# An FNet layer plus MLP on one core: shorter warm products and a re-cut opening, and two DFT weight matrices loaded in 256-byte rows

## Chip, core and metric

The kernel runs on one core of a Trainium2 chip. The metric is the device time of one execution in microseconds (us). The engines are TensorE (PE, with its weight loads shown apart as PEld), VectorE (DVE), ScalarE (ACT), GpSimd (POOL) and SyncE (SP), which here only issues DMAs.

## What is computed

The input x is 2048 rows of 640 columns. It is normalised row by row, and the normalised rows go two ways whose results are added to x:

```
xn = layernorm(x)                                   # no weights, over 640 columns
a, b = xn @ hid_re.T, xn @ hid_im.T                 # hid: 640 x 640
y  = seq_re @ a - seq_im @ b                        # seq: 2048 x 2048
out = x + y + gelu(xn @ w1 + b1) @ w2 + b2          # w1: 640 x 1536, w2: 1536 x 640
```

All data are 32-bit floats.

## The kernel before, in words

**Products.** Nearly every matrix product is made of three: each operand is split into a high part (`fp32r`, a copy on ACT) and a low part (what is left, a subtraction on DVE), and high x high, high x low and low x high are added up in PSUM (L278 to L280; in the first layer of the MLP L304). The helper `split` (L154 to L161) writes both parts. One product has 128 x 128 weights and 512 moving columns.

**The order** is written out by hand: the program text is each engine's order, and each engine, SP included, goes through its list without overtaking. A tile is waited for by semaphores that the language sets.

**The stages.** The MLP runs first, over blocks of 512 rows. The loop over g (L1051) goes through twelve hidden units of 128 columns for block 0 and twelve for block 1, with `hidden(g)` (15 products into bank g % 3), `gelu(g)` (ACT and DVE) and `output(g)` (15 products into five banks). Blocks 2 and 3 follow with a scheme that saves products (`head`, `mid`, `finish`), and then the sequence and hidden DFTs with another such scheme (from L1453 on).

**The opening (L653 to L771).** Four row tiles x0 to x3 of 128 x 640 are loaded, two by SP and two by ACT. PE meanwhile multiplies a zero tile (`warm_up`, L675, `NWARM` times, and once more later). For tiles 0 and 2 DVE finds the mean (`ln_stats`), for 1 and 3 ACT sums the rows (`sum_on_act`). `center` (L704) subtracts the mean into `xp`. PE transposes `xp` in pieces of 128 x 128 (`transpose_x`, L691) into five banks `tacc[j]`, one for each 128 columns; a bank is full when all four tiles have put their quarter there. `split` then makes `XT[j]` from bank j: its high part on ACT (L160), its low part on DVE (L161). w1's first unit, `W1[0]`, is split in two column parts (L726 to L729), its second, `W1[1]`, by `prep_w1(1)`. Then PE does `hidden(0)`, its 15 steps in the order of `FIRST` (a step (j, k): column piece j; k = 0 is high x high, 1 uses the low part of XT, 2 the low part of W1), and `hidden(1)`, with the steps that need W1's low part last. `hidden(2)` lets four transposes of `wide` (the row scales) run after its first step (L762 to L766).

**The DFT weights wr and wi (hid_re, hid_im).** They are taken in five column chunks j. `load_w(m, j)` (L378) loads chunk j of matrix m with four DMAs of 128-byte rows, `turn_w` (L390) transposes the 32 x 32 blocks on DVE into a tile `wt`, and `put_w` (L402) splits sums of it and stores them to DRAM through POOL's queue, for use much later. Chunks 0 and 1 (`WEARLY` = 2) are handled in the second MLP block, in six steps `prep_w(0)` to `prep_w(5)` after units 0 to 5 (`w_early`, L1048): chunk 0 is loaded at the end of the first block (`open_w`, L962), chunk 1 by `prep_w(0)`. `ZT` (L224) is a pair of 512-column buffers, which hold transposed rows of block 1 until `prep_xt` (L242) has split them (i = 9, L1077 to L1081) and rows of block 2 from `second_block(3)` on (L1001).

Of the kernel before, what the change touches and what calls it, by code (L numbers as in the profile page):

```python
# [15 lines left out]
P = 128  # L16
Q = 4
B = 32
EPS = 1e-5
NWARM = 10  # L20
# [6 lines left out]
def kernel(  # L27
# [261 lines left out]

    def hidden(g, aside=None):  # L290
# [4 lines left out]
        if g == 0:  # L295
            steps = FIRST
        if g == 1:

            steps.sort(key=lambda s: s[1] == 2)
        for n, (j, k) in enumerate(steps):  # L300
            if aside and n == ASIDE:
                aside()
            a, b = kinds[k]
            nc.tensor.matmul(  # L304
                acc, W1[i][:, a, j * P : (j + 1) * P], XT[j][:, b], start=n == 0, stop=n == len(steps) - 1
            )
# [70 lines left out]

    def load_w(m, j):  # L378

        if A["w"]:  # L380
            t = A["w"].tile([P, EB, B], F32, tag=f"wraw{m}", bufs=1, name=f"wraw{m}_{j}")
        else:
            t = A["wz"][:, m].rearrange("p (e b) -> p e b", b=B)
        A["wraw", m] = t
        v = (wr, wi)[m].rearrange("(n r) d -> r n d", r=B)
        for q in range(Q):
            s0 = q * DQ + j * B
            nc.sync.dma_start(t[q * B : (q + 1) * B], v[:, :, s0 : s0 + B])

    def turn_w(m, j):  # L390
        if A["w"]:
            t = A["w"].tile([P, D], F32, tag=f"wt{m}", bufs=1, name=f"wt{m}_{j}")
        else:
            t = A["wz"][:, 2 + m]
        A["wt", m] = t
        nc.vector.transpose(
            t.rearrange("p (c q i) -> p q c i", q=Q, i=B),
            A.pop(("wraw", m)).rearrange("p (q c) i -> p q c i", q=Q),
        )
# [20 lines left out]
    def prep_w(s):  # L420
# [4 lines left out]
        if k == 0:  # L425
            turn_w(0, j)
            turn_w(1, j)
            if j + 1 < ND and j != WEARLY - 1:
                load_w(0, j + 1)
                load_w(1, j + 1)  # L430
# [234 lines left out]
    nc.vector.memset(zeros, 0.0)  # L665
    warm = whole["as"][:, :TB]
    nc.vector.tensor_copy(warm, zeros)  # L667
# [3 lines left out]
    load_w1(1, cuts=(0, 2, ND))  # L671
# [3 lines left out]
    def warm_up():  # L675
        nc.tensor.matmul(wacc, warm[:, :P], warm, start=True, stop=True)  # L676
# [3 lines left out]
    load_w1(2)  # L680
# [41 lines left out]
    center(2, ALU.subtract, MV[:, 2, 0:1])  # L722
    sum_on_act(3)
    center(3, ALU.add, MV[:, 3, 5:6], 0, 2)
    center(3, ALU.add, MV[:, 3, 5:6], 2, ND)
    for lo, hi in ((0, 2 * P), (2 * P, D)):  # L726
        h, l = (W1[0][:, k, lo:hi] for k in range(2))
        nc.scalar.activation(h, first_w1[:, lo:hi], AF.Copy)
        nc.vector.tensor_tensor(l, first_w1[:, lo:hi], h.bitcast(F32), op=ALU.subtract)  # L729
# [12 lines left out]
    acc0 = hidden(0)  # L742
    prep_w1(1)
    acc1 = hidden(1)
# [188 lines left out]
    def first_block(i):  # L933
# [20 lines left out]
        if i == 10:  # L954
            load_xo(0)
            ln_scale(8, 4)
# [5 lines left out]
    def open_w():  # L962
# [4 lines left out]
        load_w(0, 0)  # L967
        load_w(1, 0)
# [15 lines left out]
    def second_block(i):  # L984
# [12 lines left out]
        if i == 3:  # L997
            A["zs"] = place("xc01", (P, 30 * P), F32, name="zs")
# [802 lines left out]
```

## Time and profile before

| | us |
|---|---|
| time, median of 3 runs (lowest to highest) | 851.04 (850.51 to 851.35) |
| time of the profiled execution | 850.46 |
| its span, first to last instruction | 848.7 |
| around the span | 1.8 |
| PE busy | 841.7 |
| DVE busy | 666.8 |
| ACT busy | 356.0 |

A time in the trace counts from the start of the span. A row of the timeline gives the start, the length and the engine, then line, operation, names and shape, a count where equal instructions follow one another, and in brackets how long the engine had been idle and what ended that. A row of a queue (SPq) gives the time in which DMAs were issued, not their transfer. A row of groups ends in the busy time, the mean length in ns, and the idle time before them.

### The profile page before, as it was taken

To read this page: it belongs to the slowest core of one execution; us is meant where nothing else is said; L and a number is where in the kernel's file an instruction comes from. 1 tells how busy PE (TensorE), PEld (TensorE's weight loads), DVE (VectorE), ACT (ScalarE), POOL (GpSimd) and SP (SyncE) were. 2 spreads that over 40 slices of the span, in tenths; PEclk is the share of its full clock that TensorE was granted. 3 is DMA by queue.
4 is the path that set the end of the run, shared out by engine and by line. 5 is a ranking of instruction groups with operands and counts; after the bars stand their busy time and mean duration, and the time that the engine had idled before them with its cause. 6 is when DMAs were issued, how large, how long until landed. Compare 5 with 4: busy or idle time off the path is not lost.

```text
span 848.7 us, 10340 instructions
## 1 busy us (share of the span) xinstructions
PE 841.7 (99%) x3707; PEld 695.2 (82%) x3707; DVE 666.8 (79%) x841; ACT 356.0 (42%) x499; POOL 48.9 (6%) x70
## 2 busy tenths in 40 slices
PE   9999999999999999999999999999999999999997
PEld 7888888878888888888888888888888888888886
DVE  6665766776758888779988887889967898885687
ACT  7454534456665555343444344232323433223241
POOL 0000311031221400000000000000000000000001
PEclk9999999999999999999999999999999999999999
DMA  6667699837679989858644679663865779705464
GB/s 182 192 184 188 159 228 252 193 87 189 202 245 355 358 186 174 173 132 188 152 137 111 162 229 289 151 150 98 205 168 169 253 191 229 306 19 180 124 172 108
DMA packets 207491, 158.45 MB, mean 187 GB/s; under 512 B 81040, under 2 KB 180880, under 8 KB 206928
## 3 DMA queue, kind: packets, MB, share of 16 engines
q1 hardware_dynamic: 198752, 135.25, 62.7%
q0 software_dynamic: 4144, 21.24, 6.3%
q10 hardware_dynamic: 4544, 1.31, 0.6%
q8 instruction: 29, 0.48, 0.3%
q14 instruction: 22, 0.18, 0.1%
HBM read 114.76 MB, written 42.99 MB: 186 GB/s over the span
## 4 chain that ended last, share of the span: by engine, by line
PE 99%; DVE 0%; issue 0%
PE banks L278 29%; PE banks L279 29%; PE banks L280 29%; PE banks L304 10%; PE banks L676 1%; PE banks L693 0%; PE banks L336 0%; PE banks L339 0%; PE banks L337 0%; DVE yo L1766 0%; DVE zeros L665 0%; DVE as L667 0%; PE banks L764 0%
## 5 line engine op out<-in xcount | busy, mean ns | idle before, releaser
L278 PE MATMUL banks<-as,xab 128*128 128x512 f32 x411 | 159.9, 389 | 0.0
L280 PE MATMUL banks<-as,xab 128*128 128x512 f32 x411 | 159.9, 389 | 0.0
L279 PE MATMUL banks<-as,xab 128*128 128x512 f32 x411 | 159.9, 389 | 0.0
L160 ACT ACTIVATE as<-r 128x1024 fp32r<-128x1024 f32 x80 | 85.0, 1062 | 178.1 <-PE banks L280 149.7
L161 DVE TENSOR_TENSOR as<-r,as 128x1024 fp32r<-128x1024 f32 x80 | 97.2, 1216 | 41.5 <-ACT as L160 41.5
L278 PEld LDWEIGHTS banks<-as,xab 128*128 128x128 f32 x411 | 77.1, 188 | 16.1
L279 PEld LDWEIGHTS banks<-as,xab 128*128 128x128 f32 x411 | 77.1, 188 | 16.0
L280 PEld LDWEIGHTS banks<-as,xab 128*128 128x128 f32 x411 | 77.1, 188 | 16.0
L278 PE MATMUL banks<-as,xc 128*128 128x512 f32 x224 | 87.1, 389 | 0.0
L279 PE MATMUL banks<-as,xc 128*128 128x512 f32 x224 | 87.1, 389 | 0.0
L280 PE MATMUL banks<-as,xc 128*128 128x512 f32 x224 | 87.1, 389 | 0.0
L160 ACT ACTIVATE as<-rt 128x1024 fp32r<-128x1024 f32 x32 | 34.0, 1062 | 70.5 <-PE banks L280 62.5
L304 PE MATMUL banks<-xtt,xab 128*128 128x512 f32 x240 | 57.1, 391 | 0.0
L304 PEld LDWEIGHTS banks<-xtt,xab 128*128 128x128 f32 x240 | 44.7, 188 | 9.8 <-ACT xtt L160 0.4
L278 PEld LDWEIGHTS banks<-as,xc 128*128 128x128 f32 x224 | 42.0, 188 | 8.8
L279 PEld LDWEIGHTS banks<-as,xc 128*128 128x128 f32 x224 | 42.0, 188 | 8.7
L280 PEld LDWEIGHTS banks<-as,xc 128*128 128x128 f32 x224 | 42.0, 188 | 8.7
L161 DVE TENSOR_TENSOR as<-rt,as 128x1024 fp32r<-128x1024 f32 x32 | 38.8, 1211 | 5.3 <-ACT as L160 5.3
L160 ACT ACTIVATE as<-u 128x1024 fp32r<-128x1024 f32 (+1 forms) x24 | 22.1, 920 | 48.2 <-PE banks L280 48.2
L512 DVE STREAM_TRANSPOSE r<-raw 128x1024 f32<-128x1024 f32 x32 | 39.5, 1240 | 3.1 <-PE banks L280 2.6
L161 DVE TENSOR_TENSOR as<-u,as 128x1024 fp32r<-128x1024 f32 (+1 forms) x24 | 24.9, 1042 | 18.8 <-ACT as L160 18.8
L512 DVE STREAM_TRANSPOSE rt<-raw 128x1024 f32<-128x1024 f32 x32 | 38.8, 1230 | 0.9 <-PE banks L280 0.8
(352 smaller groups left out, 1618.5 us busy)
## 6 DMA issues: line engine op xcount, KB each, us to landing
raw<-in_A_dft_seq_re_dram SPq DMA_DIRECT2D x64, 256.0 KB, 5.6
raw<-in_A_dft_seq_im_dram SPq DMA_DIRECT2D x64, 256.0 KB, 5.0
ws<-wit SPq DMA_DIRECT2D x15, 384.0 KB, 5.4
xs<-x SPq DMA_DIRECT2D x64, 80.0 KB, 1.8
xo<-in_A_x_dram SPq DMA_DIRECT2D x16, 320.0 KB, 6.7
xab<-wit SPq DMA_DIRECT2D x13, 384.0 KB, 4.2
wit<-wstp POOLq DMA_DIRECT2D x12, 384.0 KB, 3.7
x<-in_A_x_dram SPq DMA_DIRECT2D x14, 320.0 KB, 4.4
```

Of the source, the lines that this page charges most:

```text
L160: nc.scalar.activation(h, s, AF.Copy)
L161: nc.vector.tensor_tensor(l, s, h.bitcast(F32), op=ALU.subtract)
L278: nc.tensor.matmul(acc, wh, mh, start=first, stop=False, skip_group_check=goes_on)
L279: nc.tensor.matmul(acc, wh, ml, start=False, stop=False, skip_group_check=goes_on)
L280: nc.tensor.matmul(acc, wl, mh, start=False, stop=last, skip_group_check=goes_on)
L304: nc.tensor.matmul(acc, W1[i][:, a, j * P : (j + 1) * P], XT[j][:, b], start=n == 0, stop=n == len(steps) - 1)
L512: nc.vector.transpose(held(pieces[g][2], u).rearrange("p c (n i) -> p c n i", i=B), r.rearrange("p n (c i) -> p c n i", i=B))
L676: nc.tensor.matmul(wacc, warm[:, :P], warm, start=True, stop=True)
```

## The change

It has two parts that have nothing to do with each other.

**The opening.**

- The zero tile of the warm products is 128 x 128 instead of 128 x 512, stays an ordinary f32 tile (the `fp32r` copy on DVE is gone), and the products are 128 x 128 x 128. There are twelve instead of ten.
- Tiles 2 and 3 are centered in two column parts each (columns of pieces 0 and 1, then 2 to 4), alternating, with the split of W1[0]'s first part between them. The split of W1[0]'s second part stands between the splits of XT[1] and XT[2].
- PE transposes tiles 2 and 3 by turns for pieces 0 and 1.
- `hidden(0)` and `hidden(1)` become `first_two`: the same 30 products into the same two banks, but two of W1[0]'s last steps (those that need the low parts of XT[3] and XT[4]) stand behind the first steps of W1[1], and in FIRST some steps change place.
- w1's second unit is loaded with four DMAs instead of eight, the third with eight instead of four.

**The DFT weights.** Chunks 0 and 1 of each matrix come together, as rows of 64 columns (256 bytes). Of wi the first 16 of 20 row blocks go into ZT, behind `load_xo(0)` in `first_block(10)`; the rest, and wr, into new tiles in `open_w`. `turn_two` transposes a chunk in five pieces instead of two instructions; for chunk 1 it moves from `prep_w(3)` to the start of `second_block(3)`.

```
-NWARM = 10
+NWARM = 12
...
-    nc.vector.memset(zeros, 0.0)
-    warm = whole["as"][:, :TB]
-    nc.vector.tensor_copy(warm, zeros)
+    nc.vector.memset(zeros[:, :P], 0.0)
...
-    load_w1(1, cuts=(0, 2, ND))
+    load_w1(1)
...
-        nc.tensor.matmul(wacc, warm[:, :P], warm, start=True, stop=True)
+        nc.tensor.matmul(wacc[:, :P], zeros[:, :P], zeros[:, :P], start=True, stop=True)
...
-    load_w1(2)
+    load_w1(2, cuts=(0, 2, ND))
...
-    FIRST = [(0, 0), (0, 2), (1, 0), (1, 2), (0, 1), (2, 0), (2, 2), (1, 1), (3, 0), (3, 2)]
-    FIRST += [(2, 1), (4, 0), (4, 2), (3, 1), (4, 1)]
+    FIRST = [(0, 0), (0, 2), (1, 0), (1, 2), (0, 1), (2, 0), (1, 1), (3, 0), (2, 2), (3, 2)]
+    FIRST += [(4, 0), (4, 2), (2, 1), (3, 1), (4, 1)]
...
+    def first_two():
+        kinds = ((0, 0), (0, 1), (1, 0))
+        second = sorted(((j, k) for j in range(ND) for k in range(3)), key=lambda s: s[1])
+        order = [(0, s) for s in FIRST[:13]] + [(1, s) for s in second[:2]]
+        order += [(0, FIRST[13]), (1, second[2]), (0, FIRST[14])] + [(1, s) for s in second[3:]]
...
-    center(2, ALU.subtract, MV[:, 2, 0:1])
     sum_on_act(3)
-    center(3, ALU.add, MV[:, 3, 5:6], 0, 2)
-    center(3, ALU.add, MV[:, 3, 5:6], 2, ND)
-    for lo, hi in ((0, 2 * P), (2 * P, D)):
+    def split_first(lo, hi):
         h, l = (W1[0][:, k, lo:hi] for k in range(2))
         nc.scalar.activation(h, first_w1[:, lo:hi], AF.Copy)
         nc.vector.tensor_tensor(l, first_w1[:, lo:hi], h.bitcast(F32), op=ALU.subtract)
+    def centers(j0, j1):
+        center(2, ALU.subtract, MV[:, 2, 0:1], j0, j1)
+        center(3, ALU.add, MV[:, 3, 5:6], j0, j1)
+    centers(0, 2)
+    split_first(0, 2 * P)
+    centers(2, ND)
     transpose_x(0, 0, ND)
     transpose_x(1, 0, ND)
     warm_up()
-    for j0, j1 in ((0, 2), (2, ND)):
-        transpose_x(2, j0, j1)
-        transpose_x(3, j0, j1)
+    for j in range(2):
+        transpose_x(2, j, j + 1)
+        transpose_x(3, j, j + 1)
+    for c in (2, 3):
+        transpose_x(c, 2, ND)
     for j in range(ND):
         split(XT[j][:, 0], XT[j][:, 1], tacc[j])
+        if j == 1:
+            split_first(2 * P, D)
...
-    acc0 = hidden(0)
     prep_w1(1)
-    acc1 = hidden(1)
+    acc0, acc1 = first_two()
...
+    def load_two(m, k0=0):
+        v = (wr, wi)[m].rearrange("(n r) d -> r n d", r=B)
+        for t, n0, n1 in TWO[m][k0:]:
+            for q in range(Q):
+                nc.sync.dma_start(t[q * B : (q + 1) * B], v[:, n0:n1, q * DQ : q * DQ + 2 * B])
...
+            TWO[1] = [(ZT.rearrange("p a (e b) -> p (a e) b", b=2 * B), 0, WCUT)]
+            load_two(1)
```

The first place is DVE's list at the opening (`x_114` to `x_120` are x0, x2 and x3; `xab_122` is W1[0] and then W1[1], `xtt` is XT). Before:

```order
L665 MEMSET zeros 128x512
L667 CAST as<-zeros 128x512
...
L705 TENSOR_SCALAR xp<-x_118,mv 128x4x5x32
L705 TENSOR_SCALAR xp<-x_120,mv 128x4x2x32
L705 TENSOR_SCALAR xp<-x_120,mv 128x4x3x32
L729 TENSOR_TENSOR xab_122<-w1r_139,xab_122 128x256
L729 TENSOR_TENSOR xab_122<-w1r_139,xab_122 128x384
L161 TENSOR_TENSOR xtt<-banks,xtt 128x512 x5
```

Changed:

```order
L700 MEMSET zeros 128x128
...
L738 TENSOR_SCALAR xp<-x_118,mv 128x4x2x32
L738 TENSOR_SCALAR xp<-x_120,mv 128x4x2x32
L760 TENSOR_TENSOR xab_122<-w1r_138,xab_122 128x256
L738 TENSOR_SCALAR xp<-x_118,mv 128x4x3x32
L738 TENSOR_SCALAR xp<-x_120,mv 128x4x3x32
L161 TENSOR_TENSOR xtt<-banks,xtt 128x512 x2
L760 TENSOR_TENSOR xab_122<-w1r_138,xab_122 128x384
L161 TENSOR_TENSOR xtt<-banks,xtt 128x512 x3
```

The columns of pieces 0 and 1 of x2 and x3 are centered back to back, and the second half of W1[0] stands inside the five splits of XT.

The second place is ACT's list at the same point. Before:

```order
L728 ACTIVATE xab_122<-w1r_139 128x256
L728 ACTIVATE xab_122<-w1r_139 128x384
L160 ACTIVATE xtt<-banks 128x512 x5
L160 ACTIVATE xab_122<-w1r_148 128x640
L702 ACTIVATE ab,mv<-xp 128x640 x2
```

Changed:

```order
L759 ACTIVATE xab_122<-w1r_138 128x256
L160 ACTIVATE xtt<-banks 128x512 x2
L759 ACTIVATE xab_122<-w1r_138 128x384
L160 ACTIVATE xtt<-banks 128x512 x3
L160 ACTIVATE xab_122<-w1r_147 128x640
L735 ACTIVATE ab,mv<-xp 128x640 x2
```

Here too the second half of W1[0] moves between XT[1] and XT[2].

The third place is SP's list around the change of block. Before:

```order
L363 DMA xo_842<-in_A_x_dram 32x16x160 x4
L203 DMA xs<-x_657 32x640 x4
...
L388 DMA wraw_0_919<-in_A_dft_hid_re_dram 32x20x32 x4
L388 DMA wraw_0_924<-in_A_dft_hid_im_dram 32x20x32 x4
...
L234 DMA z_1018<-xs 32x16x160 x4
L388 DMA wraw_1_1033<-in_A_dft_hid_re_dram 32x20x32 x4
L388 DMA wraw_1_1038<-in_A_dft_hid_im_dram 32x20x32 x4
L203 DMA xs<-x_873 32x640 x4
```

Changed:

```order
L376 DMA xo_844<-in_A_x_dram 32x16x160 x4
L399 DMA zt<-in_A_dft_hid_im_dram 32x16x64 x4
L203 DMA xs<-x_659 32x640 x4
...
L399 DMA wrest<-in_A_dft_hid_im_dram 32x4x64 x4
L399 DMA wraw<-in_A_dft_hid_re_dram 32x10x64 x8
...
L234 DMA z_1028<-xs 32x16x160 x4
L203 DMA xs<-x_879 32x640 x4
```

Four DMAs into ZT stand ahead of the stores of the normalised rows (`xs`), twelve instead of eight at the end of the block, and the eight behind `z` are gone.

More of the change, by code (lines that the diff above doesn't have):

```diff
@@ L288, in unit @@
         return g if g < NF else LATE[g % NF]
+    def first_two():
[3 more added lines that the diff above has]
+        order += [(0, FIRST[13]), (1, second[2]), (0, FIRST[14])] + [(1, s) for s in second[3:]]
+        for g, (j, k) in order:
+            a, b = kinds[k]
+            ends = FIRST if g == 0 else second
+            nc.tensor.matmul(
+                bank(g),
+                W1[g][:, a, j * P : (j + 1) * P],
+                XT[j][:, b],
+                start=(j, k) == ends[0],
+                stop=(j, k) == ends[-1],
+            )
+        return bank(0), bank(1)
     def hidden(g, aside=None):
@@ L390, in turn_w @@
     def turn_w(m, j):
[L391 to L395, printed above, removed]
+        t = A["wt", m] = A["wz"][:, 2 + m]
         nc.vector.transpose(
@@ L424, in prep_w @@
             return
-        if k == 0:
+        if k == 0 and j == 0:
+            turn_two(1, j)
+            turn_two(0, j)
+        if k == 0 and j >= WEARLY:
             turn_w(0, j)
             turn_w(1, j)
-            if j + 1 < ND and j != WEARLY - 1:
+            if j + 1 < ND:
                 load_w(0, j + 1)
@@ L966, in open_w @@
         A["wst"] = A["w"].tile([P, 12 * P], F32R, name="wst")
-        load_w(0, 0)
-        load_w(1, 0)
+        t = A["w"].tile([P, EB, 2 * B], F32, name="wraw")
+        TWO[0] = [(t[:, : EB // 2], 0, EB // 2), (t[:, EB // 2 :], EB // 2, EB)]
+        TWO[1].append((A["w"].tile([P, EB - WCUT, 2 * B], F32, name="wrest"), WCUT, EB))
+        load_two(1, 1)
+        load_two(0)
     def open_tw():
```

27 lines of the change are left out of this document (19 added, 8 removed).

## Prediction

> **What bounds the kernel now.** I read the page first: which engine is busy, and what the chain that ended last is made of.
>
> ```profile
> PE 841.7 (99%) x3707; PEld 695.2 (82%) x3707; DVE 666.8 (79%) x841; ACT 356.0 (42%) x499; POOL 48.9 (6%) x70
> PE 99%; DVE 0%; issue 0%
> ```
>
> PE is busy for all but 7 us of 848.7, and the chain hardly leaves it. So an edit moves the time only where PE waits, or where it works slowly. The second view is the list of what PE's weight loads waited for, over the whole run (total, times, longest):
>
> ```profile
> PEld banks L676 <- DVE as L667: 1.9, 1, 1.9
> PEld banks L693 <- issue: 0.6, 1, 0.6
> PEld banks L304 <- ACT xtt L160: 0.4, 2, 0.2
> PEld banks L278 <- ACT banks L857: 0.3, 1, 0.3
> PEld banks L278 <- DVE banks L452: 0.3, 1, 0.3
> PEld banks L279 <- DVE xtt L161: 0.3, 1, 0.3
> PEld banks L304 <- ACT xab L160: 0.2, 1, 0.2
> ```
>
> That is all: 3.1 us in the opening (L676, L693, L304) and 0.9 us at the start of the later blocks (L278, L279). None of these names a load of wr or wi (`wraw`) or a transpose of them (`wt`). So the half of the change on the DFT weights can hardly gain; it can only cost, if it makes a new wait. What there is to gain stands in the opening. The third view is PE's timeline there:
>
> ```profile
> 1.91 4.63 PE L676 MATMUL banks<-as 128*128 128x512 f32 x10 [1.91 <-DVE as L667]
> 6.42 1.66 PE L693 MATMUL banks<-ident,xp 128*128 128x128 f32 x7
> 8.48 1.14 PE L693 MATMUL banks<-ident,xp 128*128 128x128 f32 x9
> 9.66 7.46 PE L304 MATMUL banks<-xtt,xab 128*128 128x512 f32 x31
> 16.96 0.60 PE L764 MATMUL banks<-ident,ab 128*128 128x128 f32 x4
> ```
>
> Ten warm products take 4.63, so 0.43 each (the last one's tail lies beyond). Then come transposes: seven in 1.66, over 0.2 apart; from 8.48 on nine in 1.14, 0.11 apart. **PE doubles its pace near 7.8**, 5.9 us after its first product, in the middle of the first ten transposes. The real products begin at 9.66 and run 0.23 apart; 30 of them would take 6.8, and the 31st, which opens `hidden(2)`, starts 0.23 before the transposes at 16.96, at 16.73. So only some 0.27 is lost among the 30, and the rest of the opening's price is the 9.66 us before them. That date, and the losses behind it, are what the first half of the change can move.
>
> **The opening, step by step.** DVE and ACT there, and the lengths of the centering parts from the rows by form:
>
> ```profile
> 0.91 0.48 DVE L665 MEMSET zeros<- 128x512 f32 x1 [0.91 <-PEq L1787]
> 1.43 0.43 DVE L667 CAST as<-zeros 128x512 fp32r<-128x512 f32 x1
> 5.72 0.56 DVE L705 TENSOR_SCALAR xp<-x,mv 128x640 f32<-128x640 f32 x1
> 7.38 1.15 DVE L705 TENSOR_SCALAR xp<-x,mv 128x640 f32<-128x640 f32 x3
> 9.03 0.56 DVE L729 TENSOR_TENSOR xab<-w1r,xab 128x384 fp32r<-128x384 f32 x1 [0.16 <-ACT xab L728]
> 9.63 3.08 DVE L161 TENSOR_TENSOR xtt<-banks,xtt 128x512 fp32r<-128x512 f32 x5
> ```
>
> ```profile
> L705 DVE TENSOR_SCALAR xp<-x,mv 128x384 f32<-128x384 f32 x1 | 0.4, 415 | 0.0
> L705 DVE TENSOR_SCALAR xp<-x,mv 128x256 f32<-128x256 f32 x1 | 0.3, 349 | 0.0
> ```
>
> ```profile
> 8.47 0.53 ACT L728 ACTIVATE xab<-w1r 128x384 fp32r<-128x384 f32 x1 [0.77 <-DMA w1r<-in_B_w_dram]
> 9.01 2.56 ACT L160 ACTIVATE xtt<-banks 128x512 fp32r<-128x512 f32 x5
> 9.01 0.60 ACT L160 ACTIVATE xtt<-banks 128x512 fp32r<-128x512 f32 x1
> 12.42 0.74 ACT L160 ACTIVATE xab<-w1r 128x640 fp32r<-128x640 f32 x1 [0.86 <-DMA w1r<-in_B_w_dram]
> ```
>
> *Start.* The memset is a quarter as wide; between nothing saved (0.48) and a quarter (0.12) I take 0.15, and the 0.43 of the cast goes. PE starts near 1.15 instead of 1.91, **0.75 earlier**.
>
> *Twelve short warm products.* The trace has no f32 product of 128 columns. The nearest rows bound it: a transpose of that shape (0.21 at the slow pace) and the product of 512 columns (0.43). I take 0.43: a transpose only moves data, and already takes twice as long per column as the 512-column product (0.43/512), so a true f32 product lies above it. Twelve then end near 1.15 + 5.15 = 6.3, where the first transposes can start anyway (x0 is centered at 5.72 + 0.56 = 6.28). At 0.21 they end at 3.7 and PE idles for 2.7: that is the second rival. The Trainium skill, page "FP8 and Floating Point Precision", section "TensorE Precision Notes", gives true FP32 four passes; 4 x 128 columns would be as long as the 512 of before, and the sum would stay as it is.
>
> *First ten transposes.* They start at 6.42 as before. What they take depends on when the pace doubles. I assume that the date follows PE's first work, so 0.75 earlier, near 7.05: then three transposes go at 0.21 and seven at 0.11 and end 0.35 earlier, and with the same product between (L676 there too) the second batch can start at **8.13 instead of 8.48**. Its input is ready: tile 2's and 3's first parts are centered by 7.38 + 0.35 + 0.35 = 8.08 at the latest.
>
> *First high part.* In before it starts at 9.01, 0.53 after 8.48. Bank 0 is now full after the second transpose of the batch instead of the third, 0.11 sooner: 8.55. The first product follows 0.65 later as before (9.66 - 9.01): **9.20 instead of 9.66**. W1[0]'s second half, which held ACT until 9.0, no longer stands ahead.
>
> *New stall.* That half (0.53) now stands between the high parts of XT[1] and XT[2]. High parts are 0.49 apart ((2.56 - 0.60) / 4), so XT[2]'s is ready 0.49 + 0.49 + 0.53 + 0.60 = 2.1 after the first one's start. The sixth product needs it and could start at 0.65 + 5 x 0.23 + 0.11 = 1.9, where 0.11 is what a first product after a wait loses (two starts at 9.66 and 9.99 in the trace, 0.1 over the usual 0.23). So PE waits 0.2 and loses 0.1 again. DVE does as much work as before, in another order; its last low part ends near 12.7 as it did (9.63 + 3.08), and two steps that need the last low parts now stand at places 16 and 18, behind it. W1[1] comes sooner, since the wait of 0.86 at 12.42 was for its DMAs:
>
> ```profile
> 1.65 11.02 SPq L256 DMA_DIRECT2D w1r<-in_B_w_dram  x20
> w1r<-in_B_w_dram SPq DMA_DIRECT2D x4, 80.0 KB, 2.0
> ```
>
> Each issue takes 0.5, so four fewer ahead bring it 2 us forward; it is there when ACT comes to it, near 11.5.
>
> *Sum.* From the first product: 6.8 + 0.2 + 0.2 = 7.2 (before 7.07). `hidden(2)` starts at 9.20 + 7.2 = **16.4 instead of 16.73: 0.3 us saved.** If the doubling stays at 7.8, the start is 9.55 and the sum 16.75: nothing. If it comes before 6.4, centering is the limit (second batch at 7.8 for piece 0 of tile 2, 8.1 for tile 3) and 0.5 is saved.
>
> *Does it last?* Behind the opening the next that could be late are the row scales (`wide`) and the first unit's gelu:
>
> ```profile
> 16.09 0.62 ACT L755 ACTIVATE ab<-mv 128x512 f32<-128x512 f32 x1
> 19.58 0.63 ACT L326 ACTIVATE hs<-ab 128x512 fp32r<-128x512 f32 x1
> 20.59 0.39 PE L336 MATMUL banks<-hs,rt 128*128 128x512 f32 x1
> ```
>
> `wide` ends at 16.71, 0.25 ahead of its use, and `hs` at 20.21, 0.38 ahead of PE. Both hang on ACT's list, which gains by W1[1] coming up to 0.9 earlier, so they move along. From there PE is never idle until the 0.9 us of the later blocks, and those waits hang on work that PE itself releases. So 0.3 of the opening is 0.3 at the end.
>
> **The DFT weights.**
>
> ```profile
> 86.65 1.92 SPq L363 DMA_DIRECT2D xo<-in_A_x_dram  x4
> 95.00 7.36 SPq L203 DMA_DIRECT2D xs<-x  x16
> 104.77 4.32 SPq L388 DMA_DIRECT2D wraw<-in_A_dft_hid_re_dram  x4
> ```
>
> ```profile
> 87.39 0.69 DVE L161 TENSOR_TENSOR xtt<-zt,xtt 128x512 fp32r<-128x512 f32 x1 [0.19 <-ACT xtt L160]
> 111.70 0.84 DVE L396 STREAM_TRANSPOSE wt<-wraw 128x640 f32<-128x640 f32 x1 [3.83 <-DMA wraw<-in_A_dft_hid_re_dram]
> 114.22 0.85 DVE L396 STREAM_TRANSPOSE wt<-wraw 128x640 f32<-128x640 f32 x1 [1.68 <-DMA wraw<-in_A_dft_hid_im_dram]
> ```
>
> The DMAs into ZT must wait until its last reader is done (87.39 + 0.69 = 88.1). On SP the `xs` stores are queued behind them, which start only at 95.0, when DVE has their rows. So 88.1 + 4 issues of 0.5 to 1.1 (1.92 / 4; 4.32 / 4) ends by 92.5: hidden in SP's idle 6 us. At the end of the block, twelve issues with half as many rows for the same bytes replace eight, and DVE's waits (3.8 and 1.7) can only shrink or grow by an us or two. ACT and DVE wait there, PE doesn't: nothing. Six more transposes of small size cost DVE some 0.5 for two chunks, beside PE's products: nothing. In the second block eight issues (8.4 us of SP) go, which lets `xs` and `z` of the last block come earlier; no wait of PE hangs on them: nothing. Cost of the whole half: 0, and 1 to 2 us if the cover in SP's queue were gone.
>
> **The sum against the time.** The profiled execution took 850.46, so the change gives 850.15 on its footing. The median shown is 0.6 above that execution. The Trainium skill, page "TensorE: Matmul & The Clock Gate", section "Part 1: The HAM clock gate", says that the pace doubles at the edge of a free-running window of 3.4 us, so at another date in each run; by it the first rival would hold in some runs and the 0.5 in others. One trace cannot show that: it has one doubling, 5.9 us after PE's start. I cannot tell whether the median's 0.6 stays, take half of it, and forecast **850.4**.
>
> **Rivals.** (1) *No gain*: the doubling stays at 7.8, or ACT's inserted half costs more than 0.2. `hidden(2)` then starts at 16.7 to 16.9 and the time is that of before, 850.5 to 851.1. For it speaks that only one trace shows the doubling; against it that PE starts 0.75 earlier. (2) *Slower, by the warm products*: if one takes only 0.21, they end at 3.7, PE idles for 2.7, and the doubling, 5.9 after the next work at 6.42, comes at 12.3. From 9.8 on the products would run at 0.43 for 2.5 us, a loss of 1.25; the transposes lose 0.5 more. The time is 852.2. It decides from a doubling later than the first product, 9.6. Against it: the argument on the length above. (3) *Slower, by SP's queue*: the DMAs into ZT hold up the `xs` stores after all and PE meets a wait of 1 to 3 us at the head of the later blocks: 852.5. Against it: 2.5 us of room, and no wait of PE near. (4) *Much faster* would need all of PE's later waits to go: 850.15 - 0.9 = 849.2, and even that is within the bound below.
>
> **How the numbers follow.** About 0.2% (1.7 us) is what a measurement of this kernel can tell from no change. Forecast with its spread (saving 0 to 0.8) 0.65, no gain 0.22, rival 2 0.08, rival 3 0.03, faster than all I can name 0.02. Both of the first two and 0.02 of rival 2 are within the bound: same 0.89; slower 0.09; faster 0.02. The range for 8 in 10 takes the forecast from its best case (0.5 saved, and 0.3 for the medians: 849.7) to the upper end of no gain with some spread: 851.4.
>
> **What would show it.** PE's first product at 1.1 to 1.2; twelve warm products 0.43 apart; the first product of W1[0] at 9.2; a gap of some 0.2 before the sixth; `hidden(2)` at 16.4; PE's waits from there on the same three. Warm products at 0.2, or slow transposes behind 8.5, would prove the forecast wrong, and so would a wait of PE on `z`, `xs` or `wt`.

## Result: 1.3 us slower, and two halves that cost nothing alone

The changed kernel takes 851.96 us (median of 14 runs, 850.71 to 854.75), the kernel before 850.67 (14 runs, 850.29 to 852.14): a ratio of 1.0018, 95% interval 1.0011 to 1.0025. Forecast was 850.4. The runs of the changed kernel spread over 4 us, those of before over less than 2; this spread turns out to be part of the answer.

The profiled run took 853.18 (span 851.4) and is one of the longer ones. PE's timeline in the opening, changed kernel:

```profile
1.04 5.49 PE L709 MATMUL banks<-zeros 128*128 128x128 f32 x24 [1.04 <-DVE zeros L700]
6.44 1.48 PE L726 MATMUL banks<-ident,xp 128*128 128x128 f32 x10
7.98 1.60 PE L726 MATMUL banks<-ident,xp 128*128 128x128 f32 x10
9.34 7.09 PE L299 MATMUL banks<-xtt,xab 128*128 128x512 f32 x30
16.27 0.40 PE L317 MATMUL banks<-xtt,xab 128*128 128x512 f32 x1
```

`hidden(2)` starts at 16.27 instead of 16.73; forecast was 16.4. What PE's weight loads waited for over the whole run (the five longest: total, times, longest), and the page's busy times and chain:

```profile
PEld banks L278 <- ACT hs L339: 1.1, 1, 1.1
PEld banks L709 <- DVE zeros L700: 1.0, 1, 1.0
PEld banks L279 <- DVE hs L341: 0.9, 1, 0.9
PEld banks L317 <- ACT xab L160: 0.9, 1, 0.9
PEld banks L317 <- DVE xab L161: 0.6, 1, 0.6
```

```profile
PE 843.3 (99%) x3722; PEld 696.5 (82%) x3722; DVE 666.3 (78%) x847; ACT 355.4 (42%) x499; POOL 48.9 (6%) x70
PE 84%; DMA 6%; DVE 3%; SPq 2%; issue 2%; ACT 2%; POOL 0%; ACTq 0%; DVEq 0%; POOLq 0%
```

Behind the opening the waits for `hs` and `xab` are new, and the chain that ended last, 99% PE before, now leaves PE for 16% of the span. Read the count behind PE too: 3722 records instead of 3707. The two places in PE's timeline:

```profile
30.97 2.31 PE L317 MATMUL banks<-xtt,xab 128*128 128x512 f32 x7 [0.46 <-ACT xab L160]
151.35 0.50 PE L278 MATMUL banks<-hs,r 128*128 128x512 f32 x1 [0.65 <-ACT hs L339]
152.43 0.50 PE L279 MATMUL banks<-hs,r 128*128 128x512 f32 x1 [0.58 <-DVE hs L341]
```

From start to start, PE lost 1.1 us in `hidden(4)` near 31 and 1.8 at 151. With the 0.46 gained, and what else differs along the run, the last product ends 2.7 later than in before's profile (846.27 instead of 843.56), as much as the two profiled times differ.

*The first place.* W1[4], which `hidden(4)` needs, is split on ACT behind gelu work that follows the split of W1[3], and that one waits for a DMA. ACT's timeline, first of before, then of the changed kernel:

```profile
21.39 0.74 ACT L160 ACTIVATE xab<-w1r 128x640 fp32r<-128x640 f32 x1 [0.70 <-DMA w1r<-in_B_w_dram]
29.48 0.72 ACT L160 ACTIVATE xab<-w1r 128x640 fp32r<-128x640 f32 x1
```

```profile
22.11 0.74 ACT L160 ACTIVATE xab<-w1r 128x640 fp32r<-128x640 f32 x1 [2.15 <-DMA w1r<-in_B_w_dram]
30.19 0.72 ACT L160 ACTIVATE xab<-w1r 128x640 fp32r<-128x640 f32 x1
```

PE came 0.46 earlier, the DMA 0.7 later, and W1[4] follows the DMA: 29.48 became 30.19.

*The second place.* `hs` at 151 is a unit's gelu result; ACT makes its high part behind three copies into `wst`, the buffer from which chunk 1 of wr and wi is stored. ACT's timeline, before, then changed:

```profile
141.88 0.42 ACT L160 ACTIVATE wst<-wt 128x256 fp32r<-128x256 f32 x1 [2.00 <-DMA wit<-wst]
144.56 0.63 ACT L326 ACTIVATE hs<-ab 128x512 fp32r<-128x512 f32 x1
```

```profile
147.27 0.42 ACT L160 ACTIVATE wst<-wt 128x256 fp32r<-128x256 f32 x1 [6.31 <-DMA wit<-wst]
150.67 0.63 ACT L339 ACTIVATE hs<-ab 128x512 fp32r<-128x512 f32 x1
```

A store must end before its buffer is written again; ACT stood 6.31 us for it instead of 2.00. What shared the DMA engines with it stands in the list of issues of SP, from 124 us on in before, then from 129 us on in the changed kernel:

```profile
124.12 6.00 SPq L388 DMA_DIRECT2D wraw<-in_A_dft_hid_re_dram  x4
130.23 2.39 SPq L388 DMA_DIRECT2D wraw<-in_A_dft_hid_im_dram  x4
132.72 10.72 SPq L203 DMA_DIRECT2D xs<-x  x16
144.90 2.24 SPq L234 DMA_DIRECT2D z<-xs  x4
```

```profile
129.71 8.79 SPq L203 DMA_DIRECT2D xs<-x  x16
140.91 1.92 SPq L234 DMA_DIRECT2D z<-xs  x4
142.88 2.27 SPq L845 DMA_DIRECT2D rq<-in_B_w_dram  x4
```

In before the two stores of chunk 1, issued at 138.3 and 138.9, take 3.5 and 4.3 us, and z comes behind them. In the changed kernel they are issued at 141.7 and 142.2, while z is issued (140.9 to 142.8) and ahead of rq (142.9), and take 5.5 and 7.1.

### The profile page after: what moved, and what is told of

Its sections match the earlier page's. It is cut to its first block, busy times and chain, and to the rows that moved or that the text cites. A ratio compares the mean times of both kernels' runs of the same rounds, so it can differ in the third digit from the quotient of the medians.

```text
span 851.4 us, 10375 instructions
## 1 busy us (share of the span) xinstructions
PE 843.3 (99%) x3722; PEld 696.5 (82%) x3722; DVE 666.3 (78%) x847; ACT 355.4 (42%) x499; POOL 48.9 (6%) x70
## 4 chain that ended last, share of the span: by engine, by line
PE 84%; DMA 6%; DVE 3%; SPq 2%; issue 2%; ACT 2%; POOL 0%; ACTq 0%; DVEq 0%; POOLq 0%
PE banks L279 27%; PE banks L278 27%; PE banks L280 27%; PE banks L317 2%; DMA x<-in_A_x_dram 2%; DMA wit<-wst 2%; SPq L256 1%; DMA w2r<-in_B_w_dram 1%; DMA xs<-x 1%; SPq L203 0%; ACT ab L335 0%; DVE st L185 0%; DVE x L201 0%; DVE zt L238 0%; DMA w1r<-in_B_w_dram 0%
## 5 line engine op out<-in xcount | busy, mean ns | idle before, releaser
L317 PE MATMUL banks<-xtt,xab 128*128 128x512 f32 x210 | 50.4, 391 | 0.6 <-ACT xab L160 0.5
L317 PEld LDWEIGHTS banks<-xtt,xab 128*128 128x128 f32 x210 | 39.2, 188 | 9.5 <-ACT xab L160 0.9
```

What stands on the lines that cost most here:

```text
L317: nc.tensor.matmul(acc, W1[i][:, a, j * P : (j + 1) * P], XT[j][:, b], start=n == 0, stop=n == len(steps) - 1)
```

## The experiments

Thirteen kernels ran; none changes what is computed, and where one adds work it is said. Times are medians beside runs of the kernel before on the same chip.

### Each half alone, and the queue held

`opening_only` keeps the opening and undoes the DFT half, `dft_only` the reverse. `held_queue` is the changed kernel, but `prep_w(0)` loads chunk 1 once more, over itself, with sixteen DMAs for the bytes of the eight that went (extra work), and `turn_two` for chunk 1 waits for them.

```
 opening_only: DFT part of the diff undone
 dft_only:     opening part of the diff undone
 held_queue:   + in prep_w(0): chunk 1 loaded once more, sixteen DMAs
```

> The kernel before with the whole edit of the opening and nothing of the edit on wr and wi. Theory A (the loss comes from the wr/wi half, in the second block): the saving of the opening (0.45 us at hidden(2) in the profile of the changed kernel) stays at least in part, 850.2 to 850.6 against 850.7 of before, and no wait of PE near 150 us. Theory B (the loss comes from the opening, which brings PE to the first units before their weights are there): PE waits about 1 us for W1 near 30 us, and the time is 851 to 852.

> The kernel before with the whole edit on wr and wi and nothing of the opening. Theory A: 851.2 to 852.2, with a wait of PE for a hidden unit (hs) near 148 to 150 us. Theory B: 850.7, as before, with no such wait.

> The changed kernel; at the place where chunk 1 was loaded before, chunk 1 of both matrices is loaded once more over itself, in 128-byte rows (16 DMAs, the bytes of the eight that the change removed). It adds work. Theory A with the freed queue as cause (z and w1 for the last blocks now load on top of the stores of the split weights, so ACT waits 6.3 instead of 2.0 us for a store, and PE for ACT): the stores land in 3 to 4 us again, ACT's wait near 141 us falls to 2, the wait of PE near 150 us goes, and the time is 850.3 to 851.2. If the freed queue is not the cause (the loads into ZT and the late chunk 0 are): the time stays at 852 or goes above it.

| run | this | before | ratio (95%) |
|---|---|---|---|
| opening_only | 850.64 | 850.48 | 1.0003 (0.9995 to 1.0012) |
| dft_only | 850.57 | 850.48 | 1.0002 (0.9993 to 1.0011) |
| held_queue | 855.79 | 850.48 | 1.0060 (1.0047 to 1.0073) |

Neither half alone costs anything that can be measured, so neither theory holds by itself: the two halves act together, though they were described as having nothing to do with each other. How, is seen in the slack of that `hs`: the time from the end of its low part (DVE) to the moment at which PE would start that unit's output. The low part is needed by the second product, 0.23 later, so a slack of -0.1 or -0.2 costs PE next to nothing. It is 3.5 us in before, 1.7 with the opening alone, -0.1 with the DFT half alone, -1.8 with both. The opening eats 1.8, the DFT half 3.6, together 5.3 of 3.5: in these four traces they add up, and only the sum crosses zero.

`held_queue` missed, and is no clean test: its stores did fall to 3.1 and 3.5 us, but the repeated loads became something to wait for, near 144, and PE paid twice (last section).

### What in the opening delays the second block

In the runs with the opening, DVE waits for x8, the first tile of the next block (in `held_queue` and `dft_newwarm` for x9). DVE's timeline with the opening alone:

```profile
80.66 0.89 DVE L185 BATCH_NORM_STATS2 st<-x 128x6 f32<-128x320 f32 x2 [1.27 <-DMA x<-in_A_x_dram]
```

In before that row starts at 79.27 without a wait. At the same time the list of DMA queues for a window shows a packet of 16 KB on the queue for instructions (last figure: its share of the 16 engines' time). For 77.0 to 79.6 with the opening alone, and for 79.8 to 82.0 in before:

```profile
q8 instruction: 1, 0.02, 2.5%
```

```profile
q8 instruction: 1, 0.02, 2.8%
```

2.5% of 16 engines over 2.6 us is one engine busy for 1.0 us. In before that window of 77.0 to 79.6 has no such packet: the fetch comes at 80.5, in the opening's run at 78.5. There are 29 such packets in a run, and PE has 2 x 3707 records of matmuls and weight loads, 256 for each packet. The Trainium skill, page "Perfetto Trace Analysis", section "Per-instruction lifecycle: what the profiler-reported window actually captures", says that an instruction has 64 bytes; 256 of them are 16 KB, so the trace agrees with fetches of PE's list.

The trace doesn't name the engine of a packet, so that the fetch and x8 share one is argued, not seen. A count fits it: packets under 512 B come sixteen in each 0.8 us from 79.7 to 81.3 with the opening alone, but fifteen from 78.1 to 78.9 and fifteen from 78.9 to 79.7, as if one of sixteen engines were held while the fetch runs.

The short f32 products lengthen that list: twelve products, and the one between the transposes, are 26 records of matmuls where eleven were, each with its weight load: 30 instructions more, and the 257th is reached 15 pairs, or 3.4 us at 0.227 each, earlier. That is **theory C**: the fetches move by 2 to 3 us and meet x8 instead of x11. (In the traces with the longer list the one near 80 comes 1.2 to 3.0 earlier than in before.) Theory D puts the delay to the re-ordered loads and splits.

`dft_newwarm` is `dft_only` plus the new warm products; `after_oldwarm` is the changed kernel with the old ones.

```
 dft_newwarm (on dft_only)              after_oldwarm (on the changed kernel)
-NWARM = 10                            -NWARM = 12
+NWARM = 12                            +NWARM = 10
-nc.vector.memset(zeros, 0.0)          -nc.vector.memset(zeros[:, :P], 0.0)
-nc.vector.tensor_copy(warm, zeros)    +nc.vector.memset(zeros, 0.0)
+nc.vector.memset(zeros[:, :P], 0.0)   +nc.vector.tensor_copy(warm, zeros)
 and the product's operands alike
```

> The run with the DFT half alone, and from the opening only the new warm products (short memset, no cast, twelve f32 products of 128 columns). In the runs so far hs of the unit near 150 us ended 3.5 us ahead of its use in before, 1.7 with the opening alone, 0 with the DFT half alone and 1.8 too late with both: two delays that add up and cross zero only together. Theory C says that the opening's share of that delay comes from its warm products: an f32 product takes two weight loads and two matmuls in the trace, so PE's list is longer, and each fetch of instructions (about 1 us of one DMA engine) comes 1.5 to 2.5 us earlier and falls into the load of x8 instead of x11. Then here: a fetch near 78.5 rather than 80.1, x8 landing over 1 us later than in the run with the DFT half alone (78.82), a wait of PE for hs near 150 of 1 us or more, and 851.2 to 852.0. Theory D says that the opening's share comes from the loads and splits that it re-orders (w1's units, SP's list): then the fetch may move, but x8 lands near 79, no wait over 0.3 near 150, and 850.3 to 850.8.

> The changed kernel with the warm products of before (memset of 512 columns, the copy to fp32r, ten products of 512 columns), all the rest of the change kept. Theory C: the fetches of instructions go back to where they were (one near 80 to 80.5 instead of 79.2), x8 lands near 79 to 79.5 instead of 81.42, the wait for hs near 150 is 0.3 us or nothing instead of 1.7, and the time is 850.5 to 851.0. Theory D (the re-ordered loads do it): x8 lands after 80.5, the wait near 150 stays over 1 us, and the time is 851.7 to 852.2.

`dft_newwarm` 851.99 (850.65 to 854.16), ratio 1.0015 (1.0006 to 1.0024); `after_oldwarm` 850.17 (849.97 to 850.50), ratio 0.9995 (0.9986 to 1.0004); before 850.70. **Beside the DFT half, the warm products carry the loss**: put into that half, which costs nothing by itself, they bring it; taken out of the changed kernel, it goes, and the spread with it. (Without the DFT half they cost nothing: `opening_only` has them.) In `dft_newwarm` it is x9 that comes late, not x8 as I had expected. DVE's rows for x8 and x9 there:

```profile
78.85 0.85 DVE L185 BATCH_NORM_STATS2 st<-x 128x6 f32<-128x320 f32 x2
80.94 0.89 DVE L185 BATCH_NORM_STATS2 st<-x 128x6 f32<-128x320 f32 x2 [1.00 <-DMA x<-in_A_x_dram]
```

and PE's at 150:

```profile
150.87 0.50 PE L278 MATMUL banks<-hs,r 128*128 128x512 f32 x1 [0.94 <-ACT hs L326]
151.95 0.50 PE L279 MATMUL banks<-hs,r 128*128 128x512 f32 x1 [0.58 <-DVE hs L328]
```

How a tile that is 1 us late becomes a unit that is 2 us late, is seen by putting `dft_newwarm` beside `dft_only`; behind the opening their programs are the same. Their ACT lists run 0.1 us apart from 55 us on; from x9 on `dft_newwarm` is 0.97 behind. SP's xs stores start at 95.72 instead of 94.75, and the loads of the next row tiles stand behind them in SP's queue. The second of these tiles is where it grows; DVE's row, first in `dft_only`, then in `dft_newwarm`:

```profile
106.44 0.83 DVE L185 BATCH_NORM_STATS2 st<-x 128x6 f32<-128x320 f32 x2
```

```profile
109.69 0.89 DVE L185 BATCH_NORM_STATS2 st<-x 128x6 f32<-128x320 f32 x2 [2.25 <-DMA x<-in_A_x_dram]
```

From there chunk 0's transposes, ACT's copies and `hs` are 2.0 to 2.3 late (one copy 3.2). Here too a fetch lies earlier, at 105.6 instead of 108.1; what it adds to the 1 us from x9 is not shown.

In `after_oldwarm` x8 is there in time, and PE waits 0.2 for `hs`:

```profile
78.88 0.89 DVE L185 BATCH_NORM_STATS2 st<-x 128x6 f32<-128x320 f32 x2
```

```profile
PEld banks L279 <- DVE hs L341: 0.2, 1, 0.2
```

### Is it the number of instructions?

The two runs above change three things with the products: their number in PE's list, their kind, and PE's start. Four runs were to separate these. `pad2` also cuts DVE's first memset in two, so that its small products can start at 0.94.

```
pad_oldwarm (on after_oldwarm): -NWARM = 10    +NWARM = 5, and 20 fp32r products of 128 columns
wide_f32 (on the changed kernel): -NWARM = 12  +NWARM = 5, each of 512 f32 columns
pad2 (on after_oldwarm): + eight f32 products of 32 x 32, ahead of the warm ones
wide3 (on wide_f32): -NWARM = 5                +NWARM = 3
```

> The changed kernel with the fp32r warm products of before, but five of 512 columns and twenty of 128 in the place of ten of 512: as many instructions of PE as the changed kernel has (3722 records), no f32 product, about the same length of warming. It tells the number of instructions from everything else in the short f32 products. Theory C (it is the number: fetches of instructions come earlier and fall into the loads of x8 and x9): the fetch near 80 is again at 78 to 79.3, x8 or x9 lands 1 us or more late (after 80.5), PE waits about 1 us or more for hs near 150, and the time is 851.5 to 852.2. If it is the f32 products themselves (PE's start, the clock's date, the missing copy): 850.0 to 850.5 as with the old warm products (850.17).

> The changed kernel with f32 warm products again, without the copy to fp32r, but five of 512 columns (and the single later one of 128) in the place of twelve of 128: the same kind of product and the same early start, less the wider memset, with as many instructions of PE as before the change (about 3708 records). Theory C: the fetch is back near 80, x8 to x10 land by 80.4, PE's wait for hs near 150 is 0.3 or nothing, 850.0 to 850.5. If the f32 kind matters and not the number: 851.5 to 852.2.

The times, 853.33 and 851.79 (before 850.54), answer nothing, since both openings came out too long: `hidden(2)` at 20.13 and 18.40 instead of 16.3. Measured from that start, though, the fetch and x8 went as theory C says: with the padded list the fetch is at 78.0 and x8 lands at 80.1, with the short one at 79.7 and 78.7. So the same two questions are put again with openings of the right length.

> The changed kernel with the old warm products (850.17), and ahead of them eight f32 products of 32 x 32 columns on the first columns of the zero tile, in the time in which PE waits for the copy: sixteen records of PE more, as in the changed kernel, with the opening no later. Theory C (the number of instructions shifts the fetches into the loads of x8 and x9): hidden(2) near 16.3, the fetch at 78 to 79.3 instead of 79.8, x8 or x9 1 us or more later than 78.86 and 79.61, hs of the unit near 150 0.5 us or more later than 149.47, and 850.7 to 852. If the number does nothing: x8 by 79.0, x9 by 79.8, 850.0 to 850.5.

> The changed kernel with f32 warm products, without the copy to fp32r, but three of 512 columns in the place of twelve of 128: since a pass of 512 f32 columns took 0.75 in the last run of this kind, three take 4.5 us, as long as before, and PE has 16 passes and loads of weights less than in the changed kernel. Theory C: hidden(2) at 16.0 to 16.4, the fetch near 80 or later, x8 to x10 by 80.4, no wait over 0.3 near 150, 849.9 to 850.4. If the f32 kind of the products is what does the harm: x8 late all the same and 851.5 to 852.2.

`pad2`: 850.95 (850.48 to 853.63), before 850.40, ratio 1.0010 (1.0001 to 1.0020). `wide3`: 850.04 (849.93 to 850.58), ratio 0.9996 (0.9987 to 1.0005). PE's opening and DVE's row for x8 in `pad2`:

```profile
0.94 1.06 PE L715 MATMUL banks<-zeros 128*32 128x32 f32 x16 [0.94 <-DVE zeros L700]
1.94 4.64 PE L712 MATMUL banks<-as 128*128 128x512 f32 x10
16.21 0.39 PE L317 MATMUL banks<-xtt,xab 128*128 128x512 f32 x1
```

```profile
79.92 0.89 DVE L185 BATCH_NORM_STATS2 st<-x 128x6 f32<-128x320 f32 x2 [1.24 <-DMA x<-in_A_x_dram]
```

The opening is as quick as that of `after_oldwarm`, nothing but the sixteen small records and the memset has changed, and x8 is 1.04 us late (it lands at 79.90 instead of 78.86). And `wide3` has f32 products, but few, and x8 in time:

```profile
78.82 0.88 DVE L185 BATCH_NORM_STATS2 st<-x 128x6 f32<-128x320 f32 x2
```

So the number moves the fetch, x8 comes late with the fetch, and the kind of product does no harm; nor is it PE's start, which is at 1.91 in `pad_oldwarm`, as in `after_oldwarm`. One part of my expectation of `pad2` failed: in its profiled run (850.70, one of the faster) `hs` ended at 147.37, in time and 2.1 earlier than in `after_oldwarm`. ACT's wait for the store in `pad2`:

```profile
142.19 0.42 ACT L160 ACTIVATE wst<-wt 128x256 fp32r<-128x256 f32 x1 [3.56 <-DMA wit<-wst]
```

In `after_oldwarm` that wait is 6.25. There z is issued at 138.1, 0.8 ahead of the first store of chunk 1 (138.9); in `pad2` the order is turned round, z at 138.9 and the store at 138.6. And the delay from x8 was gone on ACT before, at the copy near 129 (129.45; `after_oldwarm` 129.76). So a late x8 does not by itself bring a late `hs`: it can be swallowed by a wait for a store, and in these traces what the stores take goes with the order in which they and z are issued: 5.4 and 7.0 us in `after_oldwarm`, 3.5 and 5.2 in `pad2`. The median of `pad2` is 0.55 above that of its before, that of `after_oldwarm` 0.53 below its own; the two intervals just overlap. The runs of `pad2` reach to 853.63, so the wait may come in some of them and not in the profiled one; that is argued, not shown.

The kernels in one table, without the two with longer openings and `held_queue` (there the fetch is at 78.4 and x9 lands at 81.20, but PE waits one unit earlier). "Slack" is that of the unit near 150 us, as above. The medians come from different series, whose before lies between 850.40 and 850.70.

| kernel | PE records | hidden(2) | fetch | x8, x9 land | slack | median |
|---|---|---|---|---|---|---|
| before | 3707 | 16.73 | 80.5 | 79.19, 79.95 | 3.5 | 850.67 |
| dft_only | 3707 | 16.57 | 80.1 | 78.82, 79.64 | -0.1 | 850.57 |
| after_oldwarm | 3707 | 16.32 | 79.8 | 78.86, 79.61 | -0.1 | 850.17 |
| wide3 | 3704 | 16.30 | 80.1 | 78.79, 79.55 | -0.2 | 850.04 |
| after_best (below) | 3707 | 16.26 | 79.7 | 78.50, 79.26 | 0.5 | 850.30 |
| open_best (below) | 3707 | 16.23 | 79.8 | 78.62, 79.38 | 4.2 | 850.26 |
| opening_only | 3722 | 16.28 | 78.5 | 80.63, 81.35 | 1.7 | 850.64 |
| dft_newwarm | 3722 | 16.67 | 78.2 | 78.79, 80.91 | -2.1 | 851.99 |
| changed kernel | 3722 | 16.27 | 79.2 | 81.42, 82.21 | -1.8 | 851.96 |
| pad2 | 3723 | 16.21 | 77.7 | 79.90, 80.61 | 1.9 | 850.95 |
| held2 (below) | 3722 | 16.24 | 77.8 | 79.89, 80.53 | 2.0 | 851.16 |
| open_w1first (below) | 3722 | 15.95 | 77.5 | 79.64, 80.45 | 2.5 | 850.16 |

The split by the number of records holds in every row: with 3704 to 3707, the fetch falls on 79.7 or later, x8 is there by 79.19 and x9 by 79.95; with 3722 or 3723, the fetch falls on 79.2 or earlier and one of them lands later than that. (In the changed kernel 1.2 of its lateness is older: PE's loss near 31.) Whether it costs time is another matter: the four of them with a slack near 2 or above have medians from 0.54 below to 0.55 above their before.

### The freed queue, once more

`held2` holds SP's queue for some 6 us as the eight loads did, this time with nothing that waits for them.

```
+for m, k in ((0, 0), (0, 1), (1, 1)):   # in prep_w(0), behind the transposes of chunk 0
+    ... twelve loads of chunk 0's columns again, over themselves
```

> The changed kernel with twelve more DMAs on SP's queue, behind the second block's first transposes: they load columns that are there already once more, over themselves, and nothing waits for them. They only hold SP for some 6 us, as the eight loads did that the change took away. Extra work: 12 DMAs of 128-byte rows. Theory S (the freed queue lets xs, z and rq load beside the stores of chunk 1, and this is the larger part of the delay of hs): those stores take 3 to 4.5 us instead of 5.5 and 7.1, hs of the unit near 150 ends by 149.5 instead of 152.4, PE's wait there is 0.3 or less, and the time is 850.4 to 851.0. If the freed queue is not what delays hs: the wait of 1.7 stays, 851.8 to 852.3.

851.16 (850.20 to 852.73), ratio 1.0006 (0.9997 to 1.0015). ACT's wait in it:

```profile
142.81 0.42 ACT L160 ACTIVATE wst<-wt 128x256 fp32r<-128x256 f32 x1 [4.15 <-DMA wit<-wst]
145.61 0.63 ACT L339 ACTIVATE hs<-ab 128x512 fp32r<-128x512 f32 x1
```

The stores take 3.3 and 4.4 us again, `hs` ends at 147.32 and PE doesn't wait there. That is the mechanism as expected, in the trace. In time it is less clear: the median is 0.15 above what I gave and 0.8 under the changed kernel's, but the two intervals overlap, and the spread shows that some runs still lose. The profiled run (850.34) is one of the fastest, so where those lose is open.

### A version that keeps the gain

`open_w1first` and the two that follow load w1's fourth unit ahead of w2's second and third:

```
-load_w2(1)
-load_w2(2)
 ...
 load_w1(3)
+load_w2(1)
+load_w2(2)
```

> The run with the opening alone (850.64), with w1's fourth unit loaded ahead of w2's second and third on SP's queue. In that run the 0.45 us that the opening saves was given back near 30 us, where PE waited for the split of w1's fifth unit, which stands on ACT and DVE behind that of the fourth, whose DMAs landed at 21.4. Theory E: with the fourth unit there by 19, no such wait is left, third product of hidden(4) near 30.8 instead of 31.22, and the saving reaches the end: 850.1 to 850.3. If PE's saving is lost again further back (x8's late landing, or hs), 850.5 to 850.7. If w2, now later, is what PE waits for at output(1): 850.7 to 851.5.

> The changed kernel with the old warm products, and with w1's fourth unit loaded ahead of w2's second and third (as in the run that gave 850.16). If both repairs hold together: 849.9 to 850.2. With the old warm products the fourth unit already came early enough (20.56, no wait of PE near 30), so by theory C the re-ordered load adds little, 0.1 at most; if it moves other loads into a collision further back, 850.4 or more.

> The opening alone (DFT weights as before), with the old warm products and w1's fourth unit ahead of w2's second and third. It tells what the DFT half is worth when the opening's harm is gone: if it is worth nothing, the time is that of the changed kernel with the same repairs (849.9 to 850.2) and its margin for hs near 150 is 3 us or more; the short warm products were worth 0.1 at most on PE's start, so 850.0 to 850.2.

`open_w1first` 850.16 (849.92 to 851.14), before 850.70; `after_best` 850.30 and `open_best` 850.26, before 850.54; all three have a ratio of 0.9996 (0.9988 to 1.0005). In `open_w1first` the unit landed at 18.06 instead of 21.40, the third product of `hidden(4)` started at 30.50 instead of 31.22, and PE's wait near 30 is gone (0.33 of the difference stands at `hidden(2)` already, 15.95 instead of 16.28). The median is 0.54 under its before, that of `opening_only` 0.16 above its own. With the old warm products the unit lands at 20.56 anyway, and the re-order adds nothing. `after_best` against `open_best` says that the DFT half is worth nothing here even when nothing is in its way. No version beats the kernel before by more than the measurement tells; the largest differences are 0.54 and 0.53 (`open_w1first` and `after_oldwarm`), within their intervals.

## Why the prediction was wrong

Forecast was 850.4, no measurable change, with 0.09 for slower; it is slower by 1.3.

- **The opening came out near in size, but not by the way that was forecast.** PE's first product at 1.04 (forecast 1.15), warm products at 5.49 / 12 = 0.46 each with the tail (0.43), first real product at 9.34 (9.20), `hidden(2)` at 16.27 (16.4): 0.46 saved instead of 0.3. The forecast had the saving in a pace that doubles earlier because PE starts earlier. `dft_only` has before's opening and PE's start of before, 1.91, yet its transposes run at the fast pace from the first one on, and its first product is as early as that of the changed kernel:

```profile
6.43 1.28 PE L715 MATMUL banks<-ident,xp 128*128 128x128 f32 x10 [0.49 <-DVE xp L727]
9.35 7.62 PE L304 MATMUL banks<-xtt,xab 128*128 128x512 f32 x31
```

So the doubling at 7.8 was that of one execution. The old opening has `hidden(2)` at 16.73, 16.57 (`dft_only`) and 16.67 (`dft_newwarm`, new warm products); the re-cut one at 16.0 to 16.4 in ten traces with openings of the right length, with new and old warm products alike (`after_oldwarm` 16.32). So the re-cut saves, not the start. Beside `dft_only` it saves 0.3 in the changed kernel, all of it behind the first product: 30 products take 6.93 instead of 7.22. The forecast had 7.2 for them, with a gap before the sixth; they start 0.23 apart there, without a gap. That the sum came out near is in part luck.

- **"So 0.3 of the opening is 0.3 at the end" failed.** I looked for margins at `wide` and the first `hs` only, and held that the later waits "hang on work that PE itself releases". W1[4] hangs on a DMA: its margin was 0.18 in before (DVE ends its low part at 30.24 + 0.83 = 31.07, the third product of `hidden(4)` starts at 31.25), less than what was saved. PE coming earlier alone brings the wait of `opening_only`. In the changed kernel the DMA came 0.7 later as well; why it did (22.00, against 20.4 to 21.4 in the others) the runs do not settle.
- **The twelve short products were priced by their time alone.** 0.43 each was right and beside the point: their 30 more instructions move the fetches behind them, and x8 or x9 comes late with one of these. This stood in no term of my sum. It was to be seen: the row of warm products had x10, the product is f32 now, and the queue "instruction" stands on the page.
- **"No wait of PE hangs on them: nothing" failed**, of the eight issues that go from the second block. The earlier xs, z and rq run beside the stores of chunk 1, ACT waits for these, and `hs` stands behind on ACT. Alone, this took 3.6 of a margin of 3.5 and cost nothing that can be measured; that margin I had not looked up, since the list of waits shows only the margins that are already gone.
- **"Cost of the whole half: 0"** holds for the half alone (1.0002) and fails beside the shifted fetch. I had costed the two halves apart and added their costs; what adds up are their delays, and the cost begins where the sum exceeds the margin.
- **The rivals.** The third (SP's queue, PE waiting at the later blocks) has the right queue and nearly the right time, 852.5, but neither the place (PE waits at 150, inside the second block) nor the cause: the DMAs into ZT hold up nothing (in `dft_only` the xs stores start at 94.75, in before at 95.0). It was the queue being freed, not filled. The second (warm products at 0.21 each, PE idle behind them) did not come in the changed kernel. In `opening_only` PE did stand 1.08 ahead of the transposes, and they ran at the fast pace all the same.

## What to carry to other kernels

An edit that makes one stage earlier or frees a queue is to be weighed by the margins of what comes behind it, above all where a DMA is at the other end, and the list of waits doesn't show margins: read, for each input of the bounding engine, how long ahead of its use it is ready. Two edits that each use up part of the same margin have to be tried together. And in a kernel without slack in its loads, the count of the bounding engine's instructions is a quantity of its own, since it decides when the fetches of instructions come, and with them, by all that the traces here show, which transfer is late.

## What the runs showed of the chip

**An f32 product is two records here.** Twelve products of 128 columns are 24 rows of 0.23 us. Those of 512 f32 columns took 0.75 for each record in `wide_f32`, 1.5 for a product:

```profile
1.45 7.50 PE L712 MATMUL banks<-zeros 128*128 128x512 f32 x10 [1.45 <-DVE zeros L700]
```

**When PE's pace doubles differs between traces, and not by PE's start alone.** In before it was 5.9 us after PE's start, in `dft_only`, with the same opening, less than 4.6. The farthest is `pad_oldwarm`, with five warm products of 512 columns and twenty of 128: all twenty transposes still ran at the slow pace, until 13 us, 11 after PE's start. PE was never idle between:

```profile
4.21 4.37 PE L716 MATMUL banks<-as 128*128 128x128 f32 x20
8.37 2.35 PE L730 MATMUL banks<-ident,xp 128*128 128x128 f32 x10
10.95 2.33 PE L730 MATMUL banks<-ident,xp 128*128 128x128 f32 x10
```

The fastest run of that kernel took 850.40, which leaves no room for an opening 3.8 us longer, so it is not so in every execution. Whether the small products are the cause, one trace can't show.

**Two short waits cost a second time.** In `dft_newwarm` PE lost some 2 us at 150 and then, at full work, ran at half its pace. Columns: busy time (instructions), granted clock, DMA share, GB/s:

```profile
150.00:153.00 3.00, 1.55 (x6) 1.00 1.03 324
153.00:156.00 3.00, 3.00 (x9) 0.50 0.24 98
156.00:160.00 4.00, 4.00 (x18) 0.95 0.38 149
```

Eight products start 0.43 instead of 0.23 apart, 1.6 us more. In `held_queue` a wait of 1.79 was followed by the same from 145.8 to 149.2:

```profile
145.80:149.20 3.40, 3.40 (x10) 0.50 0.58 202
```

In the changed kernel's profiled run, waits of 0.65 and 0.58 at 151, a little shorter than the 0.94 and 0.58 of `dft_newwarm`, were not followed by it. The Trainium skill, page "TensorE: Matmul & The Clock Gate", section "Part 1: The HAM clock gate", says that the clock is granted by free-running windows of 3.4 us; the slow stretch of `held_queue` is 3.4 long, which agrees. Windows that lie differently in each run could explain why nearly the same wait costs 2 us in one run and 4 in another; that is argued, not shown. Whether the longest runs of the changed kernel (854.75) are such ones, no trace here shows.
